# Group normalization: ScalarE and VectorE in register loops over a ring, one whole tile per trip

## The chip, the cores and the metric

The kernel runs on one core of a Trainium2 chip. The metric is the device time of one execution in microseconds (us); lower is better. The span that the profile shows, from the first to the last instruction, is about 1.7 us shorter than the time of the same execution.

Engine names in the profile: PE is TensorE (matrix products) and PEld its weight loads, DVE is VectorE, ACT is ScalarE, POOL is GpSimd, SP is SyncE, which issues the large transfers. A q after the name (DVEq) is the engine's instruction sequencer.

## The reference

```python
# x: 128 x 1024 x 32 x 16 bf16; g, b: 1024 bf16; 32 groups of 32 channels
xr = x.reshape(B, G, C // G, H, W)
mu = xr.mean(axis=(2, 3, 4), keepdims=True)
var = ((xr - mu) ** 2).mean(axis=(2, 3, 4), keepdims=True)
xn = ((xr - mu) / jnp.sqrt(var + 1e-5)).reshape(B, C, H, W)
return xn * g[None, :, None, None] + b[None, :, None, None]
```

A group has 32 channels of 512 elements, 16,384 in all. One tile is 4 images x 32 groups: 128 groups on 128 partitions, 4 MB of bf16. There are 32 tiles. Each is read once and written once, 268.44 MB in all.

## The kernel before

Six tile buffers are loaded ahead. Per tile, TensorE adds up the 16,384 elements with 32 matrix products against a unit matrix, VectorE makes the mean from that, ScalarE takes two passes of squares, and then the 32 channels are scaled: VectorE does 16, GpSimd 13, ScalarE 3. Tile 0 and the last tile go in quarters, and the stores of the last two tiles do too. The parts that matter (cuts are marked `# ...`):

```python
XBUFS = 6; UPFRONT = 6; RUN = 2; QUARTERS = 4
STORE_IN_PARTS = 2; ACT_SHARE = 2; LAST_SHARE = 3; POOL_SHARE = 13
# ...
def L(i):                                   # load
    xt = xpool.tile([P, F], BF16, name="xt")
    parts = NQ if i == 0 or i >= NT - 1 else 1
    # ... one dma_start on nc.sync per part
# ...
def shifted(i):                             # squares around the first quarter's mean
    return i == 0 or i == NT - 1
# ...
def Q(i):
    # ...
    squares(st, F // 2, 0, st["negmean"][:], 1.0, s0[:])
    v0 = spool.tile([P, 1], F32, name="v0")
    finish(i - 1)                           # ScalarE's 3 scales of the tile before, its store, two loads
    # ... v0 = s0 / n + eps, on GpSimd
    squares(st, F // 2, 1, st["negmean"][:], 1.0, s1[:])
# ...
def A(i):                                   # scales
    if not in_parts(i):
        for n in range(POOL_SHARE):
            scale_on("pool", i, KC - LAST_SHARE - POOL_SHARE + n)
        for k in range(KC - LAST_SHARE - POOL_SHARE):
            scale_on("dve", i, k)
        # ...
        return
    # ... the last two tiles: a quarter scaled, a quarter stored
```

The statistics have four buffers each (`spool`, `bufs=4`), so ScalarE goes on to the next tile's squares without waiting for the scales of VectorE and GpSimd (its main wait in the trace is 61.5 us for tiles' means). The framework sets the semaphores.

## Time and profile before

| | before |
|---|---|
| time, median of 4 runs | 633.85 us (633.66 to 633.97) |
| span | 632.5 us |
| bytes moved | 268.44 MB, 424 GB/s over the span |
| ScalarE busy | 85% |
| ScalarE's time per tile when not starved | 16.7 us |
| DMA time per tile, 8.39 MB at 432 GB/s | 19.4 us |

These lines are from the page of the kernel before: the span, the busy time of each engine, the share of the 16 DMA engines and the rate in 40 slices of the span (a 9 is 90% or more), the main queue, and the chain of work that ended last, by engine.

```profile
span 632.5 us, 3907 instructions
...
PE 260.9 (41%) x1025; PEld 106.4 (17%) x1025; DVE 379.0 (60%) x645; ACT 537.9 (85%) x268; POOL 345.3 (55%) x523
...
DMA  9999999999999999999999999999999999999996
GB/s 371 437 428 406 436 433 431 433 429 433 429 424 433 429 437 431 432 434 433 434 432 424 432 433 431 429 432 432 431 431 431 436 429 432 431 425 435 431 423 260
...
q1 hardware_dynamic: 10944, 268.44, 99.0%
...
DMA 62%; ACT 15%; PE 9%; issue 5%; DVE 3%; POOL 2%; SPq 0%; DVEq 0%; ACTq 0%; POOLq 0%
```

The DMA engines stand at 9 in every slice but the last, and the rate is near 432 GB/s throughout. So the kernel is bound by its bytes.

From the page's groups of instructions (line, engine, operation, output and input; then total busy us and the mean ns of one; then the idle time ahead and what ended it):

```profile
L244 ACT ACTIVATE ja<-xt,negmean 128x8192 fp8e5<-128x8192 bf16 x60 | 426.6, 7109 | 55.2 <-DVE jd L189 55.1
L166 PE MATMUL pa<-xt,eye 128*128 128x512 bf16 x976 | 250.1, 421 | 317.9 <-DMA xt<-in_x_dram 317.9
L368 DVE TENSOR_SCALAR xt<-xt,scl,bia 128x512 bf16<-128x512 bf16 x536 | 351.4, 730 | 39.8 <-POOL bia L353 39.8
L368 POOL TENSOR_SCALAR xt<-xt,scl,bia 128x512 bf16<-128x512 bf16 x390 | 307.5, 801 | 3.4 <-POOL bia L353 0.3
```

TensorE idles 317.9 us for loads, half of the span, which fits. A scale takes VectorE 730 ns and GpSimd 801 ns on average, but that mean hides two cases. The timeline of the kernel before, near the end, shows them (start us, duration us, engine, line, operation):

```profile
574.64 11.11 DVE L368 TENSOR_SCALAR xt<-xt,scl,bia 128x512 bf16<-128x512 bf16 x16 [1.28 <-POOL bia L353]
574.71 10.24 POOL L368 TENSOR_SCALAR xt<-xt,scl,bia 128x512 bf16<-128x512 bf16 x13
...
591.62 5.26 DVE L368 TENSOR_SCALAR xt<-xt,scl,bia 128x512 bf16<-128x512 bf16 x16 [1.28 <-POOL bia L353]
```

Beside GpSimd, VectorE's 16 scales take 11.11 us, 694 ns each. A tile later GpSimd has nothing to scale, and the same 16 take 5.26 us, 329 ns each.

### The profile page before, as it was taken

What the parts mean: (1) busy time and instruction counts of PE and PEld (TensorE: products, weight loads), DVE (VectorE), ACT (ScalarE), POOL (GpSimd) and SP (SyncE); (2) the same over time, 40 slices, a digit from 0 to 9 for tenths busy, and PEclk for the clock granted to TensorE, in tenths of its full rate; (3) what the DMA queues carried; (4) which work ended last, traced back from release to release, by engine and by line L of the source; (5) the groups of instructions that cost most, each with busy time, mean ns of one, the idle gap of its engine ahead of it and who ended that gap; (6) DMA issues with size and microseconds to landing.
All of it is one profiled execution on the core that took longest, in us unless ns stands there. A gap on an engine that the chain in (4) does not pass through costs nothing.

```text
span 632.5 us, 3907 instructions
## 1 busy us (share of the span) xinstructions
PE 260.9 (41%) x1025; PEld 106.4 (17%) x1025; DVE 379.0 (60%) x645; ACT 537.9 (85%) x268; POOL 345.3 (55%) x523
## 2 busy tenths in 40 slices
PE   5577609064180632806327063270723607146000
PEld 2223203021030210302113021030301203012000
DVE  1077766666676477563665636666466663657660
ACT  4599999999999699696996969969798796987960
POOL 0077776666666377563665636666365663657100
PEclk9789759668595675957759577595875958758555
DMA  9999999999999999999999999999999999999996
GB/s 371 437 428 406 436 433 431 433 429 433 429 424 433 429 437 431 432 434 433 434 432 424 432 433 431 429 432 432 431 431 431 436 429 432 431 425 435 431 423 260
DMA packets 11063, 268.70 MB, mean 425 GB/s; under 512 B 1312, under 2 KB 1312, under 8 KB 1312
## 3 DMA queue, kind: packets, MB, share of 16 engines
q1 hardware_dynamic: 10944, 268.44, 99.0%
q8 instruction: 8, 0.13, 0.1%
q14 instruction: 15, 0.12, 0.0%
q10 hardware_dynamic: 96, 0.00, 0.0%
HBM read 134.22 MB, written 134.22 MB: 424 GB/s over the span
## 4 chain that ended last, share of the span: by engine, by line
DMA 62%; ACT 15%; PE 9%; issue 5%; DVE 3%; POOL 2%; SPq 0%; DVEq 0%; ACTq 0%; POOLq 0%
DMA out_dram<-xt 40%; DMA xt<-in_x_dram 21%; ACT ja L244 13%; PE pa L166 9%; DVE xt L368 3%; ACT xt L363 2%; POOL xt L368 1%; DMA gb_b<-in_g_dram 0%; ACT rstd L308 0%; POOL scl L337 0%; POOL shift L343 0%; POOL bia L353 0%; SPq L101 0%; DVE rstd L312 0%; DVE jd L189 0%
## 5 line engine op out<-in xcount | busy, mean ns | idle before, releaser
L244 ACT ACTIVATE ja<-xt,negmean 128x8192 fp8e5<-128x8192 bf16 x60 | 426.6, 7109 | 55.2 <-DVE jd L189 55.1
L166 PE MATMUL pa<-xt,eye 128*128 128x512 bf16 x976 | 250.1, 421 | 317.9 <-DMA xt<-in_x_dram 317.9
L368 DVE TENSOR_SCALAR xt<-xt,scl,bia 128x512 bf16<-128x512 bf16 x536 | 351.4, 730 | 39.8 <-POOL bia L353 39.8
L368 POOL TENSOR_SCALAR xt<-xt,scl,bia 128x512 bf16<-128x512 bf16 x390 | 307.5, 801 | 3.4 <-POOL bia L353 0.3
L166 PEld LDWEIGHTS <-eye 128*128 128x128 bf16 x1024 | 106.3, 106 | 472.2 <-DMA xt<-in_x_dram 318.8
L337 POOL TENSOR_SCALAR scl<-gb,rstd 128x32 f32<-128x32 f32 x31 | 11.1, 358 | 220.1 <-DVE rstd L312 220.1
L189 DVE TENSOR_SCALAR_CACHE_REDUCE jd<-pa 128x512 bf16<-128x512 f32 x32 | 21.9, 684 | 113.9 <-PE pa L166 113.9
L363 ACT ACTIVATE xt<-xt,bia,scl 128x512 bf16<-128x512 bf16 x98 | 72.0, 799 | 0.8 <-DVE bia L324 0.8
L312 DVE RECIPROCAL rstd<-rstd 128x1 f32<-128x1 f32 x32 | 5.2, 163 | 72.7 <-ACT rstd L308 72.7
L244 ACT ACTIVATE ja<-xt,q 128x4096 fp8e5<-128x4096 bf16 x8 | 29.7, 3706 | 6.6 <-DVE jd L189 6.4
L343 POOL TENSOR_SCALAR shift<-scl,negmean 128x32 f32<-128x32 f32 x31 | 11.1, 358 | 3.1
L216 POOL TENSOR_SCALAR off<-negmean,q 128x1 f32<-128x1 f32 x2 | 0.9, 430 | 20.4 <-DVE jd L189 20.4
L166 PE MATMUL pb<-xt,eye 128*128 128x512 bf16 x48 | 11.0, 379 | 0.6 <-DMA xt<-in_x_dram 0.6
L244 ACT ACTIVATION_READ_ACCUMULATOR ja<-xt,negmean 128x1 f32 x60 | 11.2, 187 | 0.0
L308 ACT ACTIVATE rstd<-s,v 128x1 f32<-128x1 f32 x30 | 8.8, 294 | 2.8
L353 POOL TENSOR_TENSOR bia<-shift,gb 128x32 f32<-128x32 f32 x31 | 7.8, 251 | 2.6
L273 POOL TENSOR_SCALAR v<-s 128x1 f32<-128x1 f32 x30 | 5.7, 191 | 2.5
L308 ACT ACTIVATE rstd<-var,eps_t 128x1 f32<-128x1 f32 x2 | 0.6, 294 | 7.5 <-DVE jv L292 7.5
L156 DVE COPY gb<-gb_p 128x64 f32<-128x64 f32 x1 | 0.2, 225 | 5.5 <-PE gb_p L148 5.5
L116 ACT ACT_TABLE_LOAD x1 | 1.3, 1283 | 1.7 <-PEq L445 1.7
L189 DVE DVE_READ_ACCUMULATOR jd<-pa 128x1 f32 x32 | 2.6, 80 | 0.0
L292 DVE TENSOR_SCALAR_CACHE_REDUCE jv<-sq,seed 128x4 f32<-128x4 f32 x2 | 0.4, 214 | 2.7 <-ACT ja L244 2.7
(18 smaller groups left out, 6.1 us busy)
## 6 DMA issues: line engine op xcount, KB each, us to landing
xt<-in_x_dram SPq DMA_DIRECT2D x30, 4096.0 KB, 19.4
out_dram<-xt SPq DMA_DIRECT2D x30, 4096.0 KB, 29.3
xt<-in_x_dram SPq DMA_DIRECT2D x8, 1024.0 KB, 11.5
out_dram<-xt SPq DMA_DIRECT2D x8, 1024.0 KB, 17.9
gb_b<-in_g_dram ACTq DMA_DIRECT2D x1, 2.0 KB, 3.2
gb_b<-in_b_dram ACTq DMA_DIRECT2D x1, 2.0 KB, 5.2
```

The lines of the kernel that those rows point to most:

```text
L116: chain("act", nc.scalar.activation(out=warm[:], in_=eps_t[:], func=ACT.Sqrt))
L166: nc.tensor.matmul(out=ps[:], lhsT=eye[:], rhs=st["xt"][:, k * MMN : (k + 1) * MMN], start=(k == lo), stop=(k == hi - 1),),
L189: nc.vector.tensor_scalar(out=jd[:], in0=ps[:], scalar1=-inv_n, scalar2=seed, op0=ALU.mult, op1=ALU.add, accum_out=total[:],),
L244: nc.scalar.activation(out=ja[:, 0:w], in_=st["xt"][:, k * w : (k + 1) * w], func=ACT.Square, bias=bias, scale=scale, accum_out=sq, satura ...
L273: nc.gpsimd.tensor_scalar(out=v0[:], in0=s0[:], scalar1=inv_n, scalar2=EPS, op0=ALU.mult, op1=ALU.add,),
L308: nc.scalar.activation(out=rstd[:], in_=last_sum[:], func=ACT.Sqrt, bias=bias[:], scale=scale),
L312: chain("dve", nc.vector.reciprocal(out=rstd[:], in_=rstd[:]))
L337: nc.gpsimd.tensor_scalar(out=scl[:], in0=gam, scalar1=rstd[:], scalar2=None, op0=ALU.mult),
L343: nc.gpsimd.tensor_scalar(out=shift[:], in0=scl[:], scalar1=st["negmean"][:], scalar2=None, op0=ALU.mult,),
L353: nc.gpsimd.tensor_tensor(out=bia[:], in0=shift[:], in1=bet, op=ALU.add),
L363: inst = nc.scalar.activation(out=span, in_=span, func=ACT.Identity, bias=bia, scale=scl)
L368: inst = eng.tensor_scalar(out=span, in0=span, scalar1=scl, scalar2=bia, op0=ALU.mult, op1=ALU.add,)
```

## The change

The diff, cut to its core (`...` marks cuts; TensorE's and SyncE's programs stay written out tile by tile):

```diff
-XBUFS = 6
-UPFRONT = 6
+SLOTS = 6
-QUARTERS = 4
-STORE_IN_PARTS = 2
-ACT_SHARE = 2
-LAST_SHARE = 3
-POOL_SHARE = 13
...
+    ring = sbuf("ring", [P, SLOTS * F], BF16)
+    nm = sbuf("nm", [P, 1], F32)
...
+    block = ctx.enter_context(nc.Block())
+
+    @block.sync
+    def _(e):
+        def load(j):
+            if j >= SLOTS:
+                e.wait_ge(st[j % SLOTS], 16 * (j // SLOTS))
+            e.dma_start(out=slot(j), in_=x_v[j]).then_inc(ld[j % SLOTS], 16)
+
+        for j in range(SLOTS):
+            load(j)
+        for i in range(NT):
+            e.wait_ge(s_done, i + 1)
+            e.dma_start(out=o_v[i], in_=slot(i)).then_inc(st[i % SLOTS], 16)
+            if i % RUN == RUN - 1:
+                first = i + 1 + SLOTS - RUN
+                for j in range(first, min(first + RUN, NT)):
+                    load(j)
+        for i in range(NT - SLOTS, NT):
+            e.wait_ge(st[i % SLOTS], 16 * (i // SLOTS + 1))
...
+    @block.scalar
+    def _(e):
...
+        with nc.Fori(0, NT, 1, engines=[e.engine]) as i:
+            e.wait_ge(s_mean, i + 1)
+            for h in range(2):
+                e.activation(
+                    out=ja[:],
+                    in_=ring[:, bass.ds((i % SLOTS) * F + h * (F // 2), F // 2)],
+                    func=ACT.Square, bias=nm[:], scale=1.0,
+                    accum_out=sq[:, h : h + 1], saturate=False,
+                )
+                e.drain()
+            e.activation(
+                out=var[:], in_=sq[:, 0:1], func=ACT.Identity, bias=eps_t[:], scale=inv_n
+            )
+            e.drain()
+            e.activation(
+                out=rstd[:], in_=sq[:, 1:2], func=ACT.Sqrt, bias=var[:], scale=inv_n
+            ).then_inc(s_rstd, 1)
+
+    @block.vector
+    def _(e):
...
+        with nc.Fori(0, NT, 1, engines=[e.engine], head_slot={e.engine: 128}) as i:
+            e.wait_ge(s_rstd, i + 1)
+            e.drain()
+            e.reciprocal(out=inv[:], in_=rstd[:])
+            e.drain()
+            e.tensor_scalar(
+                out=scl[:], in0=gb[:, 0:KC], scalar1=inv[:], scalar2=None, op0=ALU.mult
+            )
+            e.drain()
+            e.scalar_tensor_tensor(
+                out=bia[:], in0=scl[:], scalar=nm[:], in1=gb[:, KC : 2 * KC],
+                op0=ALU.mult, op1=ALU.add,
+            )
+            e.drain()
+            e.wait_ge(s_sum, i + 2)
+            mean(ps[:, bass.ds(((i + 1) % 2) * MM_FREE, MM_FREE)])
+            for k in range(KC):
+                a = ring[:, bass.ds((i % SLOTS) * F + k * HW, HW)]
+                last = e.tensor_scalar(
+                    out=a, in0=a, scalar1=scl[:, k : k + 1], scalar2=bia[:, k : k + 1],
+                    op0=ALU.mult, op1=ALU.add,
+                )
+            e.drain()
+            e.sem_inc(s_done, 1)
...
-            for n in range(POOL_SHARE):
-                scale_on("pool", i, KC - LAST_SHARE - POOL_SHARE + n)
...
```

## The prediction

> **What bounds the kernel now.** DMA. Page header and queue table: 268.44 MB, 424 GB/s over the span; in the slice view the DMA engines stand at 9 in 39 of 40 slices; middle stretches move 431 to 432 GB/s.[...] 268.44 MB at 432 GB/s is 621 us; about 2 us pass before data flows, and DMA falls silent near 626 of 632.5 us. So each tile has 19.4 us of DMA (9.7 in, 9.7 out), and PE idles 318 us for loads (groups view). ScalarE, at 85%, is second: 16.7 us per tile when not starved (timeline, 50 to 90 us).

> **What the change does.** Same bytes, same order, six slots as before. GpSimd's 13 and ScalarE's 3 channel scales per tile go to VectorE, which now does 32. In the timeline VectorE's 16 scales take 11.11 us beside GpSimd but 5.26 us with GpSimd idle (328 ns each, near 591 us).[...] So 32 scales should take about 10.5 us, if the register arithmetic ahead of each hides behind 328 ns. No run shows what a register operation costs.

> The new critical loop is ScalarE to VectorE and back: mean(i+1) waits until rstd(i) has become scale and bias (there is one nm). Per tile, from the trace: two squares with accumulator reads 2 x 7.21, Identity 0.20, Sqrt 0.29, reciprocal 0.16, scl 0.24, bia 0.25, mean 0.76, handovers about 0.1: 16.4 us.[...] So about 18.1 us per tile, under the DMA's 19.4. VectorE's own trip[...] hides in it.

> **How much is critical.** Little while the loop stays below 19.4 us, but the slack is needed: tile 0 no longer comes in quarters, so its mean falls near 22 us and its store near 50 us (45 before). The compute-limited end is 22 + 32 x loop + 11 (scales) + 10 (store) + 6 (landing, end): about 628 us at 18.1; it overtakes the DMA-limited 633 at 18.3; 19 gives about 657. The last store is now one 4 MB transfer, but five stores queue ahead of it, so that costs nothing while VectorE finishes by about 622 us. Near the crossover, small DMA gaps (after the first six loads, at the end) add some us.

> **Predicted time**: 638 us, 8 in 10 between 631 and 668. Chances: faster by over 2% 0.01, within 2% 0.65, slower 0.34.

> **What would show it.** Right: VectorE scales about 330 ns apart; squares of successive tiles 18 us apart early, later 19.4 with PE waiting for loads; DMA 9 in nearly all slices; chain of waits mostly DMA. Wrong: scales 450 ns or more apart (address arithmetic[...]); gaps of 0.3 us or more at each drain;[...] DMA below 9 in the second half with squares over 19 us apart.

> **What would make it wrong.** Register or fetch costs that lift the loop over 18.5 us; each further microsecond costs 32 us. Nothing makes it faster: the bytes are the same.

The loop per tile came to about 18.1 us: the 16.4 from the trace, and on top of them the estimate for drains, waits on registers and addresses, which rested on no trace. VectorE's own trip came to 13.5 us.

## The result and the profile after

| | before | after |
|---|---|---|
| time, median | 633.85 us | 635.18 us (634.7 to 635.64, 4 runs) |
| ratio after/before, 95% interval | | 1.0022 (1.0008 to 1.0036) |
| span | 632.5 us | 633.3 us |
| the compute loop per tile, unstarved | 16.7 us | 17.43 us |

A ratio here and below is the mean time of one kernel's fast runs over that of the other's in the same rounds, so it is not quite the ratio of the medians quoted. The change costs 1.3 us, 0.2%. That is "same" at 2%, yet the interval excludes zero. The forecast was 638.

The same lines of the page, for the kernel after:

```profile
span 633.3 us, 5191 instructions
...
PE 266.9 (42%) x1005; PEld 108.2 (17%) x1025; DVE 375.3 (59%) x1189; ACT 482.1 (76%) x194; POOL 0.8 (0%) x6
...
DMA  8999999999999999999999999999999999999986
GB/s 365 431 429 422 435 428 427 428 430 433 430 427 433 433 435 435 432 433 424 433 433 425 430 430 433 432 433 437 435 433 432 437 433 430 430 429 433 430 377 272
...
q1 hardware_dynamic: 9216, 268.44, 98.7%
...
DMA 51%; ACT 33%; DVE 4%; PE 3%; issue 3%; DVEq 2%; SPq 1%; ACTq 1%
```

The bytes, the rate and the row of nines are as before; the first slice is an 8 as the first megabyte has come only at 5.8 us in place of 5.1 (packet records), and the last two slices are discussed below. ScalarE falls from 85% to 76%, and GpSimd from 345 us to almost nothing. The chain of waits puts 33% to ScalarE where it had 15% before, although the time has hardly moved. The reason is a tie: for the first part of the run ScalarE's loop of 17.43 us runs ahead of the loads and waits for nobody, so the chain follows it there. A chain names one path that was never idle; the DMA engines were never idle either in that stretch.

The groups that answer to those of before:

```profile
L161 ACT ACTIVATE ja<-ring,nm 128x8192 fp8e5 x64 | 455.8, 7122 | 118.0 <-DVE jd L189 113.3
L140 PE MATMUL ps<-ring,eye 128*128 128x512 bf16 x1004 | 266.7, 429 | 301.5 <-DMA ring<-in_x_dram 262.7
L214 DVE TENSOR_SCALAR ring<-ring,scl,bia x1024 | 333.5, 405 | 0.0
```

TensorE still waits 262.7 us for loads. The mean of a VectorE scale fell from 730 to 405 ns by this view, and there are 1024 of them in place of 536. That 405 is too high: consecutive starts lie 326 ns apart, as the timeline shows. These are the lines of one whole trip of the kernel after, from one tile's first pass of squares to the next tile's (start us, duration us; TensorE's lines left out):

```profile
76.10 10.42 DVE L214 TENSOR_SCALAR ring<-ring,scl,bia  x32
...
76.35 7.12 ACT L161 ACTIVATE ja<-ring,nm 128x8192 fp8e5 x1 [2.12 <-DVE jd L189]
...
83.38 0.19 ACT L161 ACTIVATION_READ_ACCUMULATOR ja<-ring,nm 128x1 f32 x1
83.72 7.12 ACT L161 ACTIVATE ja<-ring,nm 128x8192 fp8e5 x1
...
90.75 0.19 ACT L161 ACTIVATION_READ_ACCUMULATOR ja<-ring,nm 128x1 f32 x1
91.00 0.29 ACT L171 ACTIVATE var<-sq,eps_t 128x1 f32<-128x1 f32 x1
91.36 0.29 ACT L175 ACTIVATE rstd<-sq,var 128x1 f32<-128x1 f32 x1
91.76 0.16 DVE L199 RECIPROCAL inv<-rstd 128x1 f32<-128x1 f32 x1 [5.23 <-ACT rstd L175]
92.00 0.24 DVE L201 TENSOR_SCALAR scl<-gb,inv 128x32 f32<-128x32 f32 x1
92.31 0.25 DVE L205 SCALAR_TENSOR_TENSOR bia<-scl,nm,gb 128x32 f32<-128x32 f32 x1
92.91 0.69 DVE L189 TENSOR_SCALAR_CACHE_REDUCE jd<-ps 128x512 bf16 x1 [0.35 <-issue]
93.53 0.08 DVE L189 DVE_READ_ACCUMULATOR jd<-ps 128x1 f32 x1
...
93.77 7.12 ACT L161 ACTIVATE ja<-ring,nm 128x8192 fp8e5 x1 [2.12 <-DVE jd L189]
```

The trip is 93.77 - 76.35 = 17.42 us, and it divides into work and gaps like this:

| part | us |
|---|---|
| two passes of squares with the reading of the sum (from its start to its own end, 2 x 7.22) | 14.43 |
| `var`, `rstd` | 0.29 + 0.29 |
| reciprocal, `scl`, `bia` | 0.16 + 0.24 + 0.25 |
| mean with the reading of its sum | 0.70 |
| sum of the work | 16.4 |
| mean to first pass, between the two passes | 0.16, 0.15 |
| ahead of `var`, `rstd`, reciprocal, `scl`, `bia` (drains and hand-overs) | 0.06, 0.07, 0.11, 0.08, 0.07 |
| ahead of the mean (drain, a wait on a register's value) | 0.35 |
| sum of the gaps | 1.05 |

The 32 scales take 10.42 us, 326 ns each. The sequencer's records show what lies behind them: one fused register operation of about 57 ns ahead of each scale, started while the scale before is still running. The address arithmetic is there and costs nothing.

The end of the run is the only place where the DMA engines are visibly less busy. From the view by windows (us; busy us of each engine; then TensorE's clock, the DMA share and GB/s), first the kernel before, then the kernel after:

```profile
610.00:615.00 5.00, 0.00 (x0) 0.00 (x0) 4.64 (x15) 2.60 (x4) 0.00 (x0) 0.50 0.99 418
615.00:620.00 5.00, 0.00 (x0) 0.00 (x0) 0.00 (x0) 0.00 (x0) 0.00 (x0) 0.50 1.00 423
```

```profile
610.00:615.00 5.00, 0.00 (x0) 0.00 (x0) 5.00 (x17) 0.00 (x0) 0.00 (x0) 0.50 0.90 387
615.00:620.00 5.00, 0.00 (x0) 0.00 (x0) 3.76 (x12) 0.00 (x0) 0.00 (x0) 0.50 0.46 197
```

After the change the last tile is stored whole. Its store can only be issued when all 32 channels are scaled, at 618.8 us by the issue records, and by then the queue is nearly empty: in the 5 us from 615 on, the share falls to 0.46. Before, the quarters of the last tiles kept it at 1.00. Taken at face value this gap is 0.10 x 5 + 0.54 x 5 = 3.2 us of DMA time, more than the whole difference of 1.3 us. That was the first suspect.

### The profile page after: what moved, and what is told of

Its sections match the earlier page's. It is cut to its first block, busy times and chain, and to the rows that moved or that the text cites. A ratio compares the mean times of both kernels' runs of the same rounds, so it can differ in the third digit from the quotient of the medians.

```text
span 633.3 us, 5191 instructions
## 1 busy us (share of the span) xinstructions
PE 266.9 (42%) x1005; PEld 108.2 (17%) x1025; DVE 375.3 (59%) x1189; ACT 482.1 (76%) x194; POOL 0.8 (0%) x6
## 3 DMA queue, kind: packets, MB, share of 16 engines
q1 hardware_dynamic: 9216, 268.44, 98.7%
## 4 chain that ended last, share of the span: by engine, by line
DMA 51%; ACT 33%; DVE 4%; PE 3%; issue 3%; DVEq 2%; SPq 1%; ACTq 1%
DMA out_dram<-ring 46%; ACT ja L161 31%; DMA ring<-in_x_dram 5%; PE ps L140 3%; DVE ring L214 2%; DVE jd L189 1%; ACT rstd L175 1%; ACT var L171 1%; DVEq L218 1%; DVEq L214 1%; DVE bia L205 1%; DVE scl L201 1%; ACTq L170 0%; SPq L107 0%; SPq L101 0%
## 5 line engine op out<-in xcount | busy, mean ns | idle before, releaser
L161 ACT ACTIVATE ja<-ring,nm 128x8192 fp8e5 x64 | 455.8, 7122 | 118.0 <-DVE jd L189 113.3
L140 PE MATMUL ps<-ring,eye 128*128 128x512 bf16 x1004 | 266.7, 429 | 301.5 <-DMA ring<-in_x_dram 262.7
L214 DVE TENSOR_SCALAR ring<-ring,scl,bia x1024 | 333.5, 405 | 0.0
L140 PEld LDWEIGHTS ps<-ring,eye 128*128 128x128 bf16 x1024 | 108.1, 108 | 459.8 <-DMA ring<-in_x_dram 283.5
L189 DVE TENSOR_SCALAR_CACHE_REDUCE jd<-ps 128x512 bf16 (+1 forms) x33 | 22.8, 692 | 49.6 <-PE ps L140 40.9
L161 ACT ACTIVATION_READ_ACCUMULATOR ja<-ring,nm 128x1 f32 x64 | 11.9, 187 | 0.0
L171 ACT ACTIVATE var<-sq,eps_t 128x1 f32<-128x1 f32 x32 | 9.4, 294 | 2.2
L175 ACT ACTIVATE rstd<-sq,var 128x1 f32<-128x1 f32 x32 | 9.4, 294 | 2.2
L205 DVE SCALAR_TENSOR_TENSOR bia<-scl,nm,gb 128x32 f32<-128x32 f32 x32 | 8.0, 251 | 2.4
L201 DVE TENSOR_SCALAR scl<-gb,inv 128x32 f32<-128x32 f32 x32 | 7.7, 241 | 2.5
L133 PE MATMUL gb_p<-gb_b,rep 32*128 32x64 bf16 x1 | 0.2, 205 | 11.1 <-DMA gb_b<-in_b_dram 11.1
L133 PEld LDWEIGHTS gb_p<-gb_b,rep 32*128 32x128 bf16 x1 | 0.1, 100 | 11.1 <-issue 11.1
## 6 DMA issues: line engine op xcount, KB each, us to landing
ring<-in_x_dram SPq DMA_DIRECT2D x32, 4096.0 KB, 19.4
```

Of the source, the lines that this page charges most:

```text
L133: e.matmul(out=gb_p[:], lhsT=rep[:], rhs=gb_b[:], start=True, stop=True).then_inc(s_gbp, 1)
L140: last = e.matmul(out=ps[:, par * MM_FREE : (par + 1) * MM_FREE], lhsT=eye[:], rhs=slot(i)[:, k * MM_FREE : (k + 1) * MM_FREE], start=(k = ...
L161: e.activation(out=ja[:], in_=ring[:, bass.ds((i % SLOTS) * F + h * (F // 2), F // 2)], func=ACT.Square, bias=nm[:], scale=1.0, accum_out= ...
L171: e.activation(out=var[:], in_=sq[:, 0:1], func=ACT.Identity, bias=eps_t[:], scale=inv_n)
L175: e.activation(out=rstd[:], in_=sq[:, 1:2], func=ACT.Sqrt, bias=var[:], scale=inv_n).then_inc(s_rstd, 1)
L189: return e.tensor_scalar(out=jd[:], in0=par, scalar1=-inv_n, scalar2=None, op0=ALU.mult, op1=ALU.add, accum_out=nm[:],).then_inc(s_mean, 1)
```

## The experiments

All 14 runs were made on four chips; the kernel before, run again, had medians from 633.66 to 633.88 us. All outputs are right. The times are medians; the ratio is against the kernel before in the same rounds. "Loop" is the time of one unstarved trip, from one first pass of squares to the next.

| label | loop us | time us | ratio (95%) |
|---|---|---|---|
| r1_after_again | 17.43 | 635.05 | 1.0015 (1.0001 to 1.0028) |
| e1_last_in_halves | 17.44 | 634.51 | 1.0014 (1.0 to 1.0028) |
| e2_no_block | 17.43 | 633.91 | 1.0005 (0.9991 to 1.0018) |
| r2_no_block_again | 17.43 | 633.98 | 1.0001 (0.9988 to 1.0015) |
| e7_halves_no_block | 17.44 | 634.67 | 1.0011 (0.9997 to 1.0024) |
| e10_two_blocks | 17.43 | 635.11 | 1.0019 (1.0005 to 1.0032) |
| e6_loop_18_1 | 18.10 | 635.72 | 1.0028 (1.0015 to 1.0042) |
| e3_loop_plus1 | 18.47 | 639.57 | 1.0097 (1.0081 to 1.0112) |
| e4_loop_plus3 | 20.17 | 693.67 | 1.0944 (1.0929 to 1.0959) |
| e5_unrolled | 16.96 | 636.94 | 1.0051 (1.0038 to 1.0065) |
| b1_no_parts | 16.71 | 633.03 | 0.9988 (0.9975 to 1.0002) |
| b2_no_pool | 16.71 | 636.11 | 1.003 (1.0016 to 1.0044) |
| e8_pe_loop | 17.43 | 636.26 | 1.0036 (1.0023 to 1.005) |
| e9_pe_loop_halves | 17.44 | 636.55 | 1.0044 (1.003 to 1.0058) |

The theories, as the expectations were written against them: the cost of 1.3 us comes from the gap ahead of the last store (theory A, the first suspect); or from what surrounds the loops, the Block that starts and ends the engines' programs (theory B); or from the longer loop. Later, when kernels with the same bytes and enough slack differed by up to 3 us, theory F was added: TensorE's instruction fetches, which the pages list among the DMA queues (q8, 8 packets of 16,384 bytes), make one of these engines late. A separate question was whether the forecast's model of the crossover was right.

### The model of the crossover: a longer loop

A useless pass of squares ahead of `var`, over W columns, lengthens the critical loop and changes nothing else.

```diff
+            e.activation(
+                out=ja[:, 0:W], in_=ring[:, bass.ds((i % SLOTS) * F, W)],
+                func=ACT.Square, bias=nm[:], scale=1.0, saturate=False,
+            )
             e.activation(
                 out=var[:], in_=sq[:, 0:1], func=ACT.Identity, ...
```

W is 1024 in e3_loop_plus1, 3072 in e4_loop_plus3 and 576 in e6_loop_18_1.

> The changed kernel with one more Square over 1024 columns per tile on ScalarE, its result unused, which should lengthen the ScalarE-VectorE loop from 17.43 to about 18.55 us. My model of the end (mean of tile 0 at 23.9 us + 32 loops + 10.5 us of scales + 14.5 us from the last scale to the end of the span) makes it compute-limited: 642.5 us of span, 644 us of time. Rival: as long as the loop stays under the DMA's 19.4 us per tile, only the last two trips count (load-limited until tile 30), so the time grows by 2 x 1.1 us, to 637.4. If the loop has less influence still (all slack), 635.

> The same with 3072 columns: loop about 20.3 us, above the DMA's 19.4. The same model says 23.9 + 32 x 20.3 + 25 = 698.5 us of span, 700 us of time, ScalarE never waiting for a load, DMA slices well below 9 in the second half. Rival (the slack of six tiles takes up most of it): 655 to 665 us.

Measured: loops of 18.47 and 20.17 us, times of 639.57 and 693.67 us, spans of 637.5 and 692.1 us. Both are bound by the loop: all trips of a run are equally long, and ScalarE never waits for a load. From the page of e3_loop_plus1, the DMA row and the chain by engine:

```profile
DMA  8999999999999999999999999999999999999966
...
ACT 79%; DVE 6%; issue 5%; ACTq 3%; DVEq 2%; DMA 2%; PE 1%; SPq 0%
```

The same row and the rates for e4_loop_plus3:

```profile
DMA  8999899999999999999999999999999999934455
GB/s 366 451 423 409 335 432 406 420 417 402 421 405 430 417 417 418 403 417 422 428 408 415 411 415 410 424 422 419 407 410 419 409 426 426 416 169 182 212 242 243
```

In the second, the loads are done after 35 slices, and only the stores of the last tiles trickle out, each when its tile is ready. Its view of waits (who waited for whom: us in total, times, longest) has TensorE waiting for VectorE's mean where it waited for loads before:

```profile
PE ps L140 <- DVE jd L193: 307.7, 28, 12.6
```

The two give the slope: (692.1 - 637.5) / (20.17 - 18.47) = 32.1 us of span per us of loop, which is the number of tiles. So the prediction's "each further microsecond costs 32 us" holds. The line through them meets the span of the kernel after, 633.3 us, at a loop of 18.47 - (637.5 - 633.3) / 32.1 = 18.34 us. The prediction had 18.3. The constant of the line, 637.5 - 32 x 18.47 = 46.5 us, was put at 22 + 11 + 10 + 6 = 49, so it was 2.5 us too high, which is 0.08 us of loop.

Then the loop was set to the length that the prediction had expected, 18.1 us, which is 0.24 us short of the crossover.

> The changed kernel with the useless Square at 576 columns, to put the loop at 18.10 us, the length that the prediction named. It tells which term of the prediction made it too high. If the loop's size was at fault (the prediction's formula plus its allowance holds at 18.1), the time is about 638. If the allowance for small DMA gaps near the crossover was at fault, the time is the larger of the two limits alone: the compute line from the 18.47 us run (637.5 us of span, 32 us per us) gives 625.7 at 18.1, which is below the DMA limit, so the time stays at about 635 to 636 (the end of tile 31 still moves later by up to 1.3 us).

The timeline of e6_loop_18_1 shows two successive first passes:

```profile
77.83 7.12 ACT L161 ACTIVATE ja<-ring,nm 128x8192 fp8e5 x1 [2.12 <-DVE jd L193]
...
95.92 7.12 ACT L161 ACTIVATE ja<-ring,nm 128x8192 fp8e5 x1 [2.12 <-DVE jd L193]
```

They start 18.09 us apart. The time is 635.72 us, 0.5 us over the kernel after and 0.7 over its repetition (0.4 and 0.8 by the ratios; the intervals overlap, so this step is not clear of noise). So had the loop been as slow as predicted, the time would have been 635.7, not 638. Of the 2.8 us by which the forecast was too high, some 0.6 belong to the loop's size. The other 2.3 are the allowance for gaps near the crossover, and they don't exist: with 0.24 us of slack per tile, the DMA engines stay full (the DMA row of this run's page is a 9 in every slice but the first, an 8, and the last, a 6).

### The gap ahead of the last store

In e1_last_in_halves the last tile is stored in two halves. The loop signals each half, and only the last tile uses that.

```diff
-            e.wait_ge(s_done, i + 1)
-            e.dma_start(out=o_v[i], in_=slot(i)).then_inc(st[i % SLOTS], 16)
+            parts = PARTS if i == NT - 1 else 1          # PARTS = 2
+            for c in range(parts):
+                e.wait_ge(s_done, PARTS * (i + 1) if parts == 1 else PARTS * i + c + 1)
+                w = F // parts
+                e.dma_start(out=o_v[i][:, c * w : (c + 1) * w], ...).then_inc(...)
...
-            e.drain()
-            e.sem_inc(s_done, 1)
+                if (k + 1) % (KC // PARTS) == 0:         # inside the loop over channels
+                    e.drain()
+                    e.sem_inc(s_done, 1)
```

> The changed kernel, but the last tile's store goes in two halves, the first as soon as 16 of its 32 scales are done. The extra 1.3 us over the kernel before have two candidate homes. Theory A (gap at the end): DMA stands partly idle from about 614 to 619 us of the trace because tile 31 is done only at 618.8; the two traces run within 0.35 us of each other until 262 of 268.4 MB have moved, then the changed kernel falls 2.6 to 3.9 us behind in bytes. Under A the halves fill the gap and the time falls by 1.3 to 2.6 us, to 632.5 to 634. Theory B (end of program): the slowest DMA engine has no gap, because it is some 5 us behind the fastest, so the gap costs nothing; the extra lies after the last transfer, where the changed kernel needs 2.0 us from the last landing wait to the end of the span and the kernel before 0.95. Under B the time stays at 635.2 within 0.5 us, and the DMA gap in the trace closes or shrinks all the same.

The view by windows of e1_last_in_halves:

```profile
610.00:615.00 5.00, 0.00 (x0) 0.00 (x0) 4.79 (x16) 0.00 (x0) 0.00 (x0) 0.50 0.96 413
615.00:620.00 5.00, 0.00 (x0) 0.00 (x0) 3.31 (x11) 0.00 (x0) 0.00 (x0) 0.50 0.94 403
```

The gap is closed: 0.94 in place of 0.46. The time falls by 0.67 us against the kernel after (0.54 against its repetition), not by the 3.2 us that the gap seemed to be worth. Even this is not clear of noise: by the ratios, each against the kernel before in the same rounds, it is 0.5 and 0.1 us.

The other direction: b1_no_parts takes the parts out of the kernel before.

```diff
-STORE_IN_PARTS = 2
+STORE_IN_PARTS = 0
...
-        parts = NQ if i == 0 or i >= NT - 1 else 1
+        parts = 1
...
-        return i == 0 or i == NT - 1
+        return False
...
         A(i)
+    finish(NT - 1)
```

> The kernel before with no tile in parts: loads of tiles 0 and 31 whole, statistics of these two tiles as for the others, stores of tiles 30 and 31 whole, ScalarE's last three scales at the end. One part of the change alone. Theory B (the end of the program costs the changed kernel its time, the gap before the last store is nearly absorbed since the DMA engines end some 5 us apart): 0 to 1 us over the kernel before. Theory A (the gap costs in full): 2.5 to 3.5 us over it.

Its view by windows has such a gap:

```profile
615.00:620.00 5.00, 0.00 (x0) 0.00 (x0) 1.56 (x3) 0.00 (x0) 1.10 (x2) 0.50 0.66 282
```

It measured 633.03 us, not slower; the 0.6 to 0.8 us by which it is below the kernel before are not clear of noise. So quarters at both ends, as the kernel before had them, buy nothing here, and theory A falls from both sides.

Why is a gap of 3 us nearly free? The landing and DMA packet records of the kernel after answer it. Each load and store of 4 MB has 128 packets of 32,768 bytes there and 16 landing records, as many as there are DMA engines, so each record is taken as one engine's report that its part is done. These are the reports for a few transfers, worked out from those records:

| transfer of the kernel after | first to last engine done, us apart |
|---|---|
| first load | 0.6 |
| about the 14th | 3.6 |
| about the 30th | 5.4 |
| store of tile 30, the last but one | 6.9 (first 614.3, median 615.4, last 621.2) |
| store of tile 31, the last | 1.4 |

The engines drift apart over the run, and it is a few that fall behind: half of them are done with the store of tile 30 within 1.1 us of the first. When the first of them run dry, at 614, the last one still has 7 us of queued work. Its queue ends at 621.16, and the store of tile 31 has been issued at 618.8; the packet records show its first packet of that store begin at 621.16, while 15 others had begun at 619.6 to 619.8. So the engine that sets the end of the run is not idle at the gap; the gap is the early engines waiting for the late one. The share of busy engines, an average of 16, shows that as lost time, but the run ends with the last engine.

### The Block

In e2_no_block the programs of the engines are emitted without the Block around them. The barrier with which it ends shows in the records of the kernel after (labelled with the exit of the contexts, where the Block is closed first): TensorE drains there at 591.2 us, ScalarE at 606.3, VectorE at 619.0 and SyncE at 631.55, and from 631.70 to 631.76 a semaphore releases them. The kernel before has no records with this label.

```diff
-    block = ctx.enter_context(nc.Block())
+    def on(e):
+        return lambda f: f(e)
-    @block.sync
+    @on(nc.sync)
...                                  # and so for the four other engines
```

> The changed kernel without the Block around the five engines' programs: the same instructions, emitted straight into the program, so that the barrier with which a Block ends should be gone. Theory B (the extra time lies in the end of the program): the span's end after SyncE's last landing wait shrinks from 2.0 to about 1.0 us and the time falls by about 1 us, to 634.2. Theory A (the gap at the end costs it): no change, 635.2 within 0.4 us.

It measured 633.91 us, 1.27 us below the kernel after and level with the kernel before. As this is a small difference, both were run again on one chip, five rounds each.

> The changed kernel itself once more, as the control of this call, now in five rounds. If the kernel has a fixed time: 635.2 within 0.4 us, 1.3 us over the kernel before. If differences of a microsecond are scatter between calls or chips: anywhere from 634 to 636.5.

> The kernel without the Block once more, beside its control on the same chip. If the Block's end costs about 1 us: 0.6 to 1.2 us under the control. If the 1.1 us of its first run was scatter: within 0.4 us of the control.

They measured 635.05 and 633.98 us. So dropping the Block takes off 1.1 to 1.3 us by the medians (0.9 to 1.1 by the means), in both comparisons, and that is about what the change cost. About half of it can be located, by the time from SyncE's last wait, when the last store has landed, to the end of the span:

| kernel | last store landed | end of span | between |
|---|---|---|---|
| before | 631.56 | 632.51 | 0.95 |
| after | 631.33 | 633.34 | 2.01 |
| r1_after_again | 631.39 | 633.40 | 2.01 |
| e2_no_block | 631.30 | 632.73 | 1.43 |
| r2_no_block_again | 630.83 | 632.26 | 1.43 |
| e10_two_blocks | 630.68 | 632.90 | 2.22 |

The tail is 0.58 us shorter without the Block, in both pairs. In the first pair that is all by which the two profiled spans differ (633.34 and 632.73); in the second, where they differ by 1.14, the last store also landed 0.56 us earlier. What makes the medians differ by 1.1 to 1.3 us beyond the tail was not located. Against the kernel before, the tail after the change is 1.06 us longer, which in these executions is most of the 1.3 us; 0.48 of it stays when the Block goes. If a Block had a fixed price, a second one should cost it again. In e10_two_blocks the first Block is closed and an empty second one follows.

```diff
-    block = ctx.enter_context(nc.Block())
+    cm = nc.Block()
+    block = cm.__enter__()
...
+    cm.__exit__(None, None, None)
+    with nc.Block() as second:
+        @second.sync
+        def _(e):
+            e.nop()
```

> The changed kernel with a second, empty Block behind the first, so that the barrier with which a Block ends comes twice. If the Block's end costs about 1 us, the span from SyncE's last landing wait to the end grows from 2.0 to about 3.0 us and the time by about 1 us over the control. If it costs nothing: as the control within 0.4 us.

It measured 635.11 us, the same as its neighbour (635.05). The tail grew by 0.21 us, and the last store landed 0.7 us earlier in that execution, so even that didn't show. A fixed price per Block is therefore not what was measured, and why the first one costs 1.1 us stays open.

Halves and no Block together:

```diff
# e1_last_in_halves + e2_no_block
```

> The changed kernel with the last tile's store in halves and without the Block. The two effects measured alone were 0.6 to 0.7 us and 1.1 us against the changed kernel. If they add, the time is 633.4 us, 0.3 us under the kernel before or equal to it; if both hide behind the same slow DMA engine, 633.9 as without the Block alone.

It measured 634.67 us. Added up, the two steps should have given 633.2 to 633.4 us; in fact the halves made the kernel without a Block 0.7 us slower. Read the other way, dropping the Block gained nothing where the last store goes in halves (634.51 with it, 634.67 without), so its 1.1 to 1.3 us are shown only for the kernel that stores the last tile whole. Differences of this size don't add. That pointed to something else that varies from kernel to kernel.

### The loops written out

```diff
-        with nc.Fori(0, NT, 1, engines=[e.engine]) as i:
+        for i in range(NT):
...
-        with nc.Fori(0, NT, 1, engines=[e.engine], head_slot={e.engine: 128}) as i:
+        for i in range(NT):
```

> The changed kernel with both register loops written out (32 copies, constant addresses, waits on constants); nothing else. In the changed kernel's trace the register work that lies on the loop is three gaps: 0.17 us before the first square, 0.15 before the second, 0.35 before the mean; without it I expect 0.05, 0.07 and 0.10, so a loop of about 17.0 us in place of 17.43. If registers cost VectorE nothing in the scales, these stay 326 ns apart. The time is set by DMA, so it should stay at the changed kernel's 635.2 within 0.5 us. Rival: the loop's registers cause the 1.3 us over the kernel before: then about 633.8.

From its timeline, VectorE's scales and two successive first passes of squares:

```profile
73.35 10.44 DVE L214 TENSOR_SCALAR ring<-ring,scl,bia 128x512 bf16<-128x512 bf16 x32
73.46 7.12 ACT L161 ACTIVATE ja<-ring,nm 128x8192 fp8e5<-128x8192 bf16 x1 [1.73 <-DVE jd L189]
...
90.42 7.12 ACT L161 ACTIVATE ja<-ring,nm 128x8192 fp8e5<-128x8192 bf16 x1 [1.74 <-DVE jd L189]
```

The loop is 16.96 us, so register addresses and register waits cost 0.47 us per trip: the gap ahead of the mean falls from 0.35 to 0.10 us, the one from the mean to the first pass from 0.16 to 0.03, the one between the passes from 0.15 to 0.07. The scales take 10.44 us as against 10.42: addresses from a register neither slow them nor cost anything. So far the expectation held. But the time rose by 1.8 us, to 636.94, where a shorter loop should have changed nothing. That was a miss, and a kernel whose loop has only shorter gaps came out slower. The pages show one thing more that differs, the instruction fetches of queue q14, first the kernel after, then e5_unrolled:

```profile
q14 instruction: 2, 0.02, 0.0%
```

```profile
q14 instruction: 14, 0.11, 0.0%
```

Each fetch there is of 8,192 bytes. The loop's branch itself is short: in the records of the kernel after it lasts 45 ns on ScalarE and 56 ns on VectorE (medians), and from its start to that of the next instruction it is 0.16 and 0.20 us. What the fetches do is taken up below, under "What the remaining differences follow".

### GpSimd's scales

In b2_no_pool the kernel before gives GpSimd no scales; VectorE has 29 and ScalarE 3.

```diff
-POOL_SHARE = 13
+POOL_SHARE = 0
```

> The kernel before with GpSimd's 13 scales per tile given to VectorE (29 there, 3 stay on ScalarE): another part of the change alone. VectorE's scales go from 694 to about 328 ns apart, its 29 take about 9.5 us where 16 took 11.1. DMA sets the time, so that is worth nothing except a little at the very end: 633.7 us within 1 us. If GpSimd's traffic disturbed anything on the critical path, the time falls by more than 1 us.

Its timeline shows the 29 scales:

```profile
84.93 9.46 DVE L368 TENSOR_SCALAR xt<-xt,scl,bia 128x512 bf16<-128x512 bf16 x29 [1.28 <-POOL bia L353]
```

That is 326 ns each, where 16 beside GpSimd had taken 694 each. So GpSimd's 13 scales had cost VectorE more than they saved it: 16 and 13 side by side take 11.11 us, all 29 on VectorE 9.46. Yet the time is 2.3 us longer, 636.11. Neither the loop (16.71 us) nor any wait that was found explains it.

### What the remaining differences follow

With the loop at 18.1 us or less, all these kernels are bound by DMA and move the same bytes, but they differ by up to 3.9 us, and they repeat themselves: the two kernels that were run twice came back within 0.13 us. (Single executions of one kernel lie within 0.6 to 1.7 us of each other.) In the profiled executions the time follows one number from the DMA packet records: when the last of the 16 engines is done with the last store but one.

| kernel | last engine done with the store before the last, us | time of that profiled execution, us |
|---|---|---|
| b1_no_parts | 620.2 | 633.03 |
| r2_no_block_again | 620.7 | 633.98 |
| e10_two_blocks | 620.5 | 634.65 |
| e2_no_block | 621.1 | 634.46 |
| after, r1_after_again | 621.2 | 635.06, 635.14 |
| e6_loop_18_1 | 621.5 | 635.38 |
| e5_unrolled | 623.0 | 636.88 |
| e8_pe_loop | 623.4 | 637.26 |

The large differences go with how late the latest engine is. From there on the rest is fixed: in each of these executions that engine takes 9.7 us for its part of the last store, and after the landing comes the tail (1.0 us in b1_no_parts). The difference between the kernel after and the one without a Block is in part such lateness, 621.2 against 621.1 and 620.7, and for the rest the 0.58 us of the tail. Theory F asked why one engine is late. TensorE's program is the long one that stayed written out, and eight fetches of it, 16,384 bytes each, go through the DMA engines (queue q8 on the pages of both kernels). In e8_pe_loop TensorE loops over a register too. As its waits would then be on six load semaphores chosen by the register, GpSimd, which is idle, waits for loads and means in a written-out program and passes them on as one counter.

```diff
+    s_go = sem("go")
...
     @block.gpsimd
...
+        for i in range(NT):
+            e.wait_ge(ld[i % SLOTS], 16 * (i // SLOTS + 1))
+            if i >= 2:
+                e.wait_ge(s_mean, i - 1)
+            e.sem_inc(s_go, 1)
...
     @block.tensor
...
-        for i in range(NT):
-            e.wait_ge(ld[i % SLOTS], 16 * (i // SLOTS + 1))
-            if i >= 2:
-                e.wait_ge(s_mean, i - 1)
+        with nc.Fori(0, NT, 1, engines=[e.engine]) as i:
+            e.wait_ge(s_go, i + 1)
```

> The changed kernel with TensorE in a register loop too (one tile per trip; the idle GpSimd waits for load and free PSUM half and passes that on through one semaphore). It takes away TensorE's instruction fetches: the changed kernel's trace has eight of 16 KB during the run, and few others. In that trace the sixteen DMA engines finish one and the same store further and further apart, 0.6 us at the first transfer, 6.9 us at store 30, and the last engine to finish sets the end: SyncE issues store 31 at 618.8 us, while store 30 has landed only at 621.7. Theory F (the fetches load one DMA engine and make it the late one): the spread at store 30 falls to 2 to 4 us, store 30 lands by about 619.5, and the time falls by 1.5 to 2.5 us, to 632.7 to 633.7, then limited by the issue of store 31. Rival (the spread has another source): spread and time as in the changed kernel, 635.2 within 0.5 us. [...]

The fetches are gone: its page has no line for q8. The engines are spread by 7.2 us in the store before the last, as against 6.9, and the time rose by 1.1 us. Theory F falls, for TensorE's fetches. Where the time went can be told in part. The view by windows has one stretch in which it moves less, first the kernel after, then e8_pe_loop:

```profile
480.00:560.00 80.00, 32.48 (x125) 13.33 (x128) 48.37 (x154) 61.62 (x25) 0.00 (x0) 0.69 1.01 433
```

```profile
480.00:560.00 80.00, 32.76 (x128) 13.61 (x128) 48.09 (x154) 61.37 (x25) 0.00 (x0) 0.69 1.00 423
```

423 in place of 433 GB/s over 80 us is worth 80 x 10 / 433 = 1.8 us. (This execution took 637.26 us, 1.0 above the kernel's median and 2.2 above the profiled one of the kernel after.) The DMA share is about the same in both, so the engines were busy but moved less: a packet of 32,768 bytes took 1.240 us there on average, as against 1.215. The engines' busy times are alike. The kernel before moved 429 and b2_no_pool 425 GB/s in the same stretch.

The last run puts the looped TensorE, the halves and no Block together.

```diff
# e8_pe_loop + e1_last_in_halves + e2_no_block
```

> The same with the last tile's store in halves and without the Block. Under theory F the gap before the last store is then the limit, and the halves do pay: 630.5 to 632 us, below both kernels. Under the rival: 634 to 635 us as the halves without the Block had.

It measured 636.55 us, no better than e8_pe_loop alone. Neither of the two steps that helped by themselves helps here.

The records don't name the engine of a packet, but 99% of the data packets of the kernel after begin within 5 ns of the end of another, which is taken as the one before it on the same engine, so packets can be strung into 16 chains by matching ends with starts. (Two engines whose packets end in the same few ns can be confused. This was done from the kept traces, one execution each; no run tests it.) The chains show two things:

- In the kernel after, TensorE's eight fetches, of 0.93 to 1.03 us each, hold up eight different engines, one each, and in r1_after_again they do too. They could not have made one engine late, which is how theory F fails.
- In e5_unrolled, seven of the last eight fetches of q14 before the stores end, from 264 to 613 us, hold up one and the same engine, the one that is done last at 623.0. Each delays it by 0.30 us, and its next packet takes 1.56 to 1.84 us in place of the usual 1.21: 5.6 us in all, of the 7.9 us by which this engine trails the first. So the likely reason that writing the loops out cost time is their instruction fetches. In b1_no_parts, with 14 fetches too, they fall on several engines, and the last is done at 620.2.

What stays open: why one DMA engine falls behind in the kernel after, and why by a different amount in each of the other kernels.

None of the variants clearly beats both kernels. The nearest is b1_no_parts at 0.9988, and its interval reaches 1.0002.

## Why the prediction was right or wrong

It forecast 638 us and 4.2 us of loss; measured were 635.18 us and 1.3 us. The range (631 to 668) held the result, and "within 2%" was the likeliest class. The size of the loss was too large by a factor of three.

- **DMA bounds the kernel and goes on bounding it: right.** The same bytes, 424 GB/s over both spans, the row of nines. "Nothing makes it faster" held too: 14 runs, none clearly below the kernel before.
- **The loop: right in its mechanism, 0.7 us too long.** The work in it was put at 16.4 us and is 16.4. What is added by drains, register waits and addresses was estimated at some 1.7 us (18.1 less 16.4; from no trace) and is 1.05. The loop is 17.43, not 18.1. Lengthened to 18.10 it costs 0.5 to 0.7 us by the medians, so this error accounts for a quarter of the excess at most.
- **Scales at 328 ns, register arithmetic hidden: right.** 326 ns, 10.42 us for 32, the same written out. VectorE's own trip, predicted 13.5 us, is 12.6 and hidden.
- **The slope and the crossover: right.** 32.1 us per us was measured for "each further microsecond costs 32 us", and 18.34 for a crossover at 18.3. The start was later than before, as said: the first store is issued at 51.7 us (predicted near 50, before 45.2), tile 0's mean ends at 23.9 (predicted near 22). It costs nothing, as six loads are under way: in five stretches from 4 to 80 us the DMA share of the kernel after is 0.98 to 1.03.
- **The failed step: "Near the crossover, small DMA gaps (after the first six loads, at the end) add some us".** The prediction's own formula gave the larger of 628 and 633. The point was set at 638 on top of that with nothing worked out for the difference. The run at the predicted loop gave 635.72, so some 2.3 us of the excess are this allowance. There were no gaps after the first six loads. The one at the end exists, and closing it gave back 0.7 us at most, because the latest DMA engine works through it.
- **The last store whole: right in its conclusion, wrong in its reason.** "Costs nothing while VectorE finishes by about 622 us": VectorE finished at 618.8. But five stores were not still in the queue; the early engines had run dry at 614. It is cheap because the late engine wasn't dry. The prediction looked at the mean share of the engines here too ("DMA falls silent near 626"): in the kernel before, the last engine worked until 631.2.
- **The 1.3 us that there are: not foreseen.** They go away with the Block when the last store goes whole, and the prediction didn't mention the Block. So even the direction came out right for another reason than the one given, which is luck. The tail after the last landing is 1.06 us longer than before, of which 0.58 us go with the Block; the rest of what its removal saves was not located, a second Block adds nothing, and with the last store in halves its removal gains nothing, so this is a cause by removal in one kernel, not an explained one.

## What to carry to other kernels

When a kernel is bound by its bytes, work out at which loop length the compute takes over, and then trust the larger of the two sums: here a loop 0.24 us short of that point cost about half a microsecond, hardly clear of noise, and one 0.13 us beyond it cost 4 us. Judge a gap near the end of a run by when the last DMA engine is done, not by the mean share of all 16, since here engines that had drifted apart by 7 us hid most of a gap of 3. And treat differences of 1 or 2 us in 630 between kernels with the same traffic with suspicion even when they repeat: here they did not add up, and writing out a loop, which shortened it, cost 1.8 us, most likely by the instruction fetches of the longer program.
